# Second product of batch 2 as seven products of halves, and the whole list of steps in a new order

## The chip, the cores and the metric

One core of one Trainium2 chip. The metric is the device time of one execution in microseconds (us), the median of several runs. The core has a matrix engine (PE, with its weight loads shown apart as PEld), VectorE (DVE), ScalarE (ACT), GpSimd (POOL) and SyncE (SP), which only issues DMAs here. Each engine works through its own instructions in order; between engines only semaphores set the order.

## The reference

There are B = 8 batches of H = 8 heads, S = 512 tokens, 32 states, D = 64. Tokens read the states and states read the tokens, and the rows of both go through a two-layer network with a PReLU between.

```python
scores = scale * x @ state.T ; a = softmax(scores)  ; xread = a @ state
scores2 = scale * state @ x.T; a2 = softmax(scores2); sread = a2 @ x
rows = concat([xread, sread], axis=2)      # per batch 512 + 32 rows of d_model = 512
h = rows @ w_in                            # d_ff = 2048
g = maximum(h, 0) + alpha * minimum(h, 0)
out = g @ w_out                            # float32, 4352 x 512
```

## The kernel before

The kernel is a list of some 1,100 steps, the string `ORDER`. A step is a name with numbers, `F.5.12.2` for instance, and a small function is called for each. Every function puts instructions on one engine, so the list fixes the order on each of the five engines; there is no scheduler. A step waits for the data that it reads, and for the tile or PSUM bank that it writes to become free. PSUM banks are chosen in the list too: the last number of a PE step is one of six single banks, and a pair of banks named `two` holds the scores (`sc`) and some of the `m` products.

The token side needs no `xread`: since a @ state @ w_in = a @ (state @ w_in), the kernel forms m = state @ w_in once for each batch and then h = a @ m. Batch number 8 in the list is no batch of tokens: it holds the 32 state rows of all eight batches.

The steps, with b the batch:

- `lx`, `wi`, `wo`, `lst`: loads of x, w_in, w_out and the states, issued by POOL. `xd` (transposed x) and `tt` (transposed weights of a2) are DMA transposes, issued by SP. Batches 0 and 1 transpose x on PE (`xt`) and copy it out (`xo`); batch 0 takes its token weights through PE too (`tsc`, `at`, `ao`).
- `sc` (PE): scores into `two`. For the tokens: `sb` (DVE, transpose in blocks), `smax` (DVE), `ssh` (POOL or DVE, subtract), `sexp` (ACT), `ssum` (DVE), `snorm` (POOL), `wb` (DVE, back). After `wb` of its batch the first `F` can run. For the states: `tm` (DVE), `nb`, `te` (ACT), `tsum` (DVE), `tn` (POOL, two to a batch), `tt` (SP), `rd` (PE), `rdo` (copy). `te` is the last reader of the scores, and the next user of `two` waits for it.
- `m.b.f`: m for a quarter f of d_ff, `mo`: its copy to SBUF by ACT (`a`) or DVE (`v`).
- `F.b.j.k` (PE): a 128-wide chunk j of h, 16 to a batch, in bank k, two matmuls of 512 columns (four of 256 for batch 8). `N.b.j` (ACT): max(-h, 0). `G.b.j` (DVE): g = (1 - alpha) * N + h, which frees the bank. `f`, `n`, `g` are the same by half tokens, for the first four chunks of batch 0. `oma` is 1 - alpha.
- The second product in the plain form, for batches 0, 1 and 2: `S.b.q.i`, two of the sixteen matmuls of 512 columns that make one 128-row tile q of the output; `O.b.q`: its copy by ACT or DVE, and the DMA out from SP.
- The second product as seven products of halves (Strassen), for batches 3 to 8. g is cut in token halves and d_ff halves, w_out in d_ff halves and column halves. `W.i.c` (POOL, eight steps in all) forms the four sums of halves of w_out once. `U.b.i.c` (POOL) forms four sums of quarters of g, each in two parts c, eight steps to a batch; its tile has one buffer, so the sum of the next batch waits for the product that reads it. `P.b.p.i.c` (PE) are four matmuls of 256 columns, 28 such steps to a batch of tokens, in three banks px, py and pv. Products accumulate in px and intermediate states of it are kept: `K` (copy of px by ACT or DVE). `Q` (DVE, or a copy on ACT) adds a kept part to py or pv, and sends a quarter of the output.

```python
W_SUMS = {1: ((0, 1), (0, 0)), 3: ((1, 1), (0, 1)), 2: ((1, 1), 1), 4: ((1, 0), 2)}
# U: 1: g(1,c)+g(1,2+c)   2: U1-g(0,c)   3: g(0,c)-g(1,c)   4: g(0,2+c)-U2
```

In the trace the lines are: `F` L532 and L541 (batch 8), `S` L602, `P` L690, `m` L483, `sc` L298, `rd` L456, `N` L585, `G` L588, `U` L669, `W` L645, `K` L706, `Q` L721 and L723, `O` L619, `mo` L507 and L509, `te` L421, `tn` L435, `ssh` L367, `snorm` L384, `ssum` L380 and L381, `wb` L392, `sb` L329, `tm` L404.

Of the kernel before, what the change touches and what calls it, by code (L numbers as in the profile page):

```python
# [17 lines left out]
stc Z.0.9 wi.0 cx.0.1.a stt.0 sto.v Z.1.5 xt.0.0.1.1 lst sbd.0.v cx.0.0.a xt.0.0.0.2 xo.0.0.0.a cx.1.0.v cx.1.1.v  # L18
Z.3.6 xt.0.1.0.3 sbd.1.a lx.1 tsc.0.0.4 xo.0.0.1.v tsc.0.1 xt.0.1.1.5 sc.0.0 xo.0.1.1.a xo.0.1.0.v tsc.1.0.2 Z.0.2
tsc.1.1 smax.0.0 ssh.v.0.0 sexp.0.0 smax.0.1 ssh.v.0.1 sexp.0.1 sc.0.1 tm.0 Z.0.5 m.0.0.0.1 Z.3.11 oma mo.0.0.a.0  # L20
ssum.0.1 nb.0.a te.0.0 te.0.1 str.1.3 sro.1.a str.0.5 Z.4.13 wi.1 wo.0 snorm.p.0.1 at.1.4 ao.1.a ssum.0.0 snorm.p.0.0
sro.0.v wi.2 mo.0.0.v.1 m.2.0.2.0 mo.2.0.v.1 wo.1 m.1.0 mo.1.0.a at.0.3 ao.0.v xt.1.1.0.5 mo.2.0.v.0 wi.3 xo.1.1.0.a
xt.1.1.1.1 xo.1.1.1.v xt.1.0.1.4 xo.1.0.1.v f.0.1.1.0 n.0.1.1 g.0.1.1.1 xt.1.0.0.3 xo.1.0.0.v wo.2 f.0.0.0.2 n.0.0.0
g.0.0.0.0 m.1.1 mo.1.1.a m.0.1.5.1 mo.0.1.a.0 f.0.0.1.4 mo.0.1.a.1 g.0.1.1.0 f.0.1.0.3 W.1.0.p sc.1 n.0.0.1 n.0.1.0
g.0.0.0.1 tm.1 g.0.0.1.0 nb.1.a F.0.6.0 g.0.0.1.1 sb.1 g.0.1.0.1 N.0.6 G.0.6 g.0.1.0.0 F.0.5.2 te.1.0 lx.2 te.1.1
S.0.1.1.5 F.0.4.1 S.0.3.1.4 wo.3 S.0.3.0 S.0.1.0 m.0.2 F.0.7.0 N.0.4 G.0.4 N.0.5 G.0.5 mo.0.2.a N.0.7 S.0.2.1.3
S.0.2.0 G.0.7 F.0.9.1 tsum.1 tn.1.0 N.0.9 G.0.9 smax.1 ssh.p.1 xd.2 tsum.0 tn.0.1 F.0.10.2 S.0.3.3 N.0.10 G.0.10
S.0.1.3 tn.1.1 tt.1 S.0.1.2 F.0.8.0 F.0.11.1 N.0.11 N.0.8 S.0.3.2 G.0.8 m.0.3 S.0.0.0.2 G.0.11 S.0.2.3 S.0.0.3 S.0.0.2
mo.0.3.a tn.0.0 S.0.0.1 sexp.1 ssum.1 snorm.p.1 F.0.12.0 F.0.15.1 N.0.15 N.0.12 G.0.12 S.0.0.5 G.0.15 tt.0 S.0.0.4
S.0.1.4 m.1.2 S.0.1.5 wb.1 mo.1.2.a S.0.2.4 F.0.14.0 N.0.14 G.0.14 S.0.3.5 F.0.13.1 m.1.3 N.0.13 S.0.3.4 mo.1.3.a  # L30
F.1.3.0 N.1.3 S.0.0.7 G.0.13 S.0.0.6 O.0.0.a G.1.3 W.1.1.p F.1.4.1 N.1.4 G.1.4 S.0.2.6 F.1.2.2 N.1.2 F.1.0.0 N.1.0
G.1.2 S.0.1.6 S.0.1.7 O.0.1.a sc.2 G.1.0 tm.2 rd.0.1 m.2.2.2.5 rd.1.0 mo.2.2.a.0 W.2.0.p mo.2.2.a.1 S.0.2.2 F.1.1.2
F.1.8.5 rdo.0.v rdo.1.v nb.2.a te.2.1 N.1.8 sb.2 G.1.8 S.0.2.7 S.0.2.5 N.1.1 S.0.3.6 G.1.1 te.2.0 F.1.13.1 N.1.13 lx.3
tsum.2 S.0.3.7 O.0.3.a F.1.12.0 smax.2 F.1.6.5 G.1.13 O.0.2.a S.1.1.1.2 F.1.9.4 N.1.12 G.1.12 N.1.6 G.1.6 N.1.9
F.1.5.3 G.1.9 N.1.5 S.1.1.0 F.1.15.1 N.1.15 F.1.14.0 N.1.14 S.1.0.1.5 S.1.0.0 tn.2.0 ssh.p.2 tn.2.1 sexp.2 m.3.2
mo.3.2.a G.1.5 G.1.14 W.2.1.p m.3.0.4.3 mo.3.0.a.0 S.1.0.4 F.1.11.0 S.1.1.6 N.1.11 G.1.15 S.1.0.7 tt.2 mo.3.0.a.1
# [2 lines left out]
S.1.2.3.1 sb.3 smax.3 ssh.p.3 S.1.0.3 nb.3.a te.3.0 S.1.1.5 W.3.0.p F.2.0.0 N.2.2 te.3.1 rdo.2.v N.2.0 S.1.1.4 S.1.2.5
S.1.1.7 S.1.2.1 G.2.2 G.2.0 O.1.0.a O.1.1.a m.3.1 m.4.0.4.5 mo.4.0.a.1 m.4.1.3.2 tsum.3 mo.4.1.v.0 F.2.14.0 S.1.2.7  # L40
N.2.14 G.2.14 F.2.11.5 N.2.11 G.2.11 S.1.3.0.3 mo.4.1.a.1 S.1.3.7 F.2.9.0 S.1.3.3 mo.4.0.v.0 F.2.5.2 sexp.3 ssum.3
N.2.9 G.2.9 S.1.2.6 F.2.3.5 F.2.1.4 N.2.3 G.2.3 S.1.3.5 S.1.2.2 xd.4 mo.3.1.a S.1.3.4 N.2.1 G.2.1 N.2.5 G.2.5 F.2.8.0
lx.5 S.1.2.4 snorm.p.3 S.1.2.0 O.1.2.a wb.3 F.2.7.5 N.2.7 G.2.7 S.1.3.2 F.2.6.4 N.2.6 G.2.6 F.2.4.2 N.2.4 N.2.8
S.1.3.1 S.1.3.6 O.1.3.a F.2.10.1 sc.4 m.5.0.5.4 mo.5.0.a.1 mo.5.0.a.0 G.2.4 S.2.0.0.3 N.2.10 G.2.8 F.2.15.2 N.2.15
F.2.12.4 N.2.12 F.2.13.0 N.2.13 tm.4 F.3.9.5 G.2.10 G.2.15 S.2.0.1 G.2.13 nb.4.a S.2.2.0.1 W.3.1.p te.4.1 sb.4 W.4.1.p
te.4.0 S.2.0.4 S.2.2.5 N.3.9 G.2.12 xd.5 S.2.0.5 S.2.2.4 tn.3.0 tn.3.1 tt.3 tsum.4 m.4.2.2.0 mo.4.2.a.0 smax.4 ssh.p.4
# [1 line left out]
tn.4.1 F.3.10.5 N.3.10 G.3.10 m.5.2 mo.5.2.a rd.3.4 S.2.0.3 sexp.4 S.2.2.6 m.6.0 m.7.0.2.0 ssum.4 mo.7.0.a.1 S.2.0.6
O.2.0.a S.2.1.5.5 S.2.2.2 mo.7.0.a.0 F.3.2.0 N.3.2 G.3.2 F.3.6.3 rdo.3.a F.3.3.2 tn.4.0 tt.4 snorm.p.4 S.2.2.1 N.3.3
G.3.3 lx.6 N.3.6 F.3.8.4 F.3.0.0 S.2.2.7 F.3.11.2 G.3.6 S.2.1.4 S.2.1.2 N.3.8 G.3.8 N.3.0 G.3.0 mo.6.0.a m.5.3.3.4  # L50
N.3.11 sc.5 F.3.14.0 N.3.14 S.2.1.1 xd.6 O.2.2.v G.3.11 tm.5 F.3.4.1 mo.5.3.a.1 nb.5.a wb.4 te.5.1 mo.5.3.a.0 te.5.0
sb.5 N.3.4 G.3.14 S.2.1.3 F.3.5.2 S.2.3.2.4 W.4.0.p S.2.3.4 U.3.1.0.p G.3.4 N.3.5 G.3.5 smax.5 U.3.2.0.p U.3.4.0.p
S.2.3.3 S.2.3.6 S.2.3.7 S.2.1.0 rd.4.3 m.5.1 mo.5.1.a S.2.3.1 F.3.13.0 F.4.6.1 rdo.4.a N.3.13 G.3.13 N.4.6 F.4.1.2
F.3.12.3 S.2.3.0 G.4.6 N.3.12 N.4.1 G.4.1 G.3.12 lx.7 S.2.1.7 F.4.10.0 N.4.10 S.2.1.6 O.2.1.v F.4.4.1 N.4.4
P.3.1.1.0.2 ssh.p.5 sexp.5 P.3.1.0.1 U.3.1.1.p S.2.3.5 O.2.3.a U.3.2.1.p F.4.13.3 G.4.4 F.4.0.5 G.4.10 P.3.2.1.1.1
ssum.5 N.4.13 N.4.0 G.4.0 F.4.3.4 P.3.1.0.0 P.3.1.1.1 K.3.1.a P.3.2.0.1 P.3.2.0.0 G.4.13 N.4.3 U.3.4.1.p F.4.8.0 N.4.8
F.4.7.5 N.4.7 G.4.3 F.4.9.3 snorm.p.5 N.4.9 P.3.6.0.0 F.4.11.4 N.4.11 G.4.7 P.3.6.1.0 G.4.11 P.3.6.0.1 P.3.2.1.0
U.3.3.1.p G.4.8 P.3.6.1.1 K.3.2.a F.4.15.5 N.4.15 F.4.2.4 P.3.5.0.0 P.3.5.1.1 P.3.5.1.0 F.4.5.0 wb.5 G.4.15 P.3.5.0.1
G.4.9 Q.3.0.0 N.4.2 F.4.12.5 m.6.3.3.1 K.3.4.a P.3.3.1.0 G.4.2 U.3.3.0.p P.3.3.0.0 F.4.14.4 mo.6.3.v.1 N.4.12 G.4.12
P.3.3.1.1 N.4.5 G.4.5 N.4.14 G.4.14 mo.6.3.a.0 P.3.3.0.1 Q.3.0.1.a P.3.7.1.1.1 U.4.1.0.p U.4.2.0.p U.4.4.0.p U.4.1.1.p  # L60
m.6.2.5.0 mo.6.2.a.0 sc.6 sb.6 m.7.3.3.4 mo.7.3.a.0 m.6.1.2.5 mo.6.1.a.0 tm.6 mo.6.2.a.1 mo.6.1.a.1 P.3.7.0.0
P.3.7.1.0 P.3.7.0.1 Q.3.1.1 F.5.3.3 N.5.3 F.5.4.2 F.5.2.0 F.5.7.5 N.5.7 G.5.3 G.5.7 N.5.2 G.5.2 nb.6.a te.6.1 N.5.4
tsum.5 smax.6 G.5.4 P.3.4.1.1 P.3.4.0.0 P.4.1.1.1.3 P.4.1.1.0 F.5.14.5 N.5.14 P.4.1.0.0 P.4.1.0.1 K.4.1.a U.4.2.1.p
P.3.4.1.0 mo.7.3.a.1 P.3.4.0.1 F.5.10.0 N.5.10 F.5.13.2 N.5.13 G.5.14 F.5.1.4 G.5.10 G.5.13 tn.5.1 P.4.6.1.1 F.5.9.5
Q.3.1.0 N.5.9 tn.5.0 N.5.1 G.5.1 P.4.6.0.0 P.4.6.1.0 P.4.6.0.1 K.4.2.a P.4.2.0.0.0 te.6.0 F.5.11.2 G.5.9 tt.5 xd.7
ssh.v.6 N.5.11 G.5.11 F.5.0.1 N.5.0 F.5.15.4 P.4.5.1.0 P.4.5.0.1 N.5.15 G.5.15 F.5.8.5 U.4.3.1.p P.4.5.1.1 F.5.12.2
tsum.6 N.5.8 G.5.8 P.4.2.1.0 sexp.6 ssum.6 P.4.5.0.0 U.4.4.1.p F.5.6.4 G.5.0 P.4.2.0.1 P.4.2.1.1 K.4.4.a P.4.3.0.1
P.4.3.1.1 N.5.12 G.5.12 U.4.3.0.p P.4.7.0.0.5 N.5.6 F.5.5.1 P.4.3.1.0 P.4.3.0.0 Q.4.0.1.a snorm.p.6 U.5.1.0.p G.5.6
P.4.7.1.0 P.4.7.1.1 P.4.7.0.1 m.7.1.2.4 Q.4.0.0 wb.6 rd.5.0 sc.7 N.5.5 mo.7.1.a.0 rdo.5.a mo.7.1.a.1 G.5.5 m.7.2.3.1
mo.7.2.a.1 mo.7.2.a.0 F.6.8.2 Q.4.1.1 P.4.4.1.0 F.6.1.0 P.4.4.1.1 sb.7 N.6.1 G.6.1 F.6.12.4 F.6.3.1 N.6.3 F.6.6.3 tm.7  # L70
P.4.4.0.1 P.4.4.0.0 N.6.6 G.6.6 N.6.8 N.6.12 Q.4.1.0 P.5.1.0.1.0 nb.7.a te.7.1 tn.6.0 tn.6.1 tt.6 te.7.0 P.5.1.1.0
U.5.2.0.p G.6.3 G.6.8 U.5.1.1.p U.5.2.1.p P.5.1.0.0 tsum.7 P.5.1.1.1 K.5.1.a F.6.2.3 smax.7 tn.7.0 tn.7.1 P.5.2.1.0.5
# [702 lines left out]
```

## Time and profile before

| | us |
|---|---|
| median of 3 runs (lowest, highest) | 219.38 (219.21, 219.97) |
| the profiled execution | 219.88 |
| its span, first to last instruction | 218.1 |
| first matmul starts, last matmul ends | 1.33, 214.29 |
| busy: PE, DVE, POOL, ACT | 207.0, 171.5, 164.3, 144.4 |
| granted TensorE clock, mean | 0.998 |

"Busy" of PE counts each matmul to its modelled end, and neighbours overlap; so where the prediction speaks of PE's work it uses the distance from one matmul's start to the next one's when PE waits for nothing. An idle engine costs time only where another waits for what it does next.

### The profile page before, as it was taken

To read this page: it belongs to the slowest core of one execution; us is meant where nothing else is said; L and a number is where in the kernel's file an instruction comes from. 1 tells how busy PE (TensorE), PEld (TensorE's weight loads), DVE (VectorE), ACT (ScalarE), POOL (GpSimd) and SP (SyncE) were. 2 spreads that over 40 slices of the span, in tenths; PEclk is the share of its full clock that TensorE was granted. 3 is DMA by queue.
4 is the path that set the end of the run, shared out by engine and by line. 5 is a ranking of instruction groups with operands and counts; after the bars stand their busy time and mean duration, and the time that the engine had idled before them with its cause. 6 is when DMAs were issued, how large, how long until landed. Compare 5 with 4: busy or idle time off the path is not lost.

```text
span 218.1 us, 4862 instructions
## 1 busy us (share of the span) xinstructions
PE 207.0 (95%) x1931; PEld 128.3 (59%) x1931; DVE 171.5 (79%) x258; ACT 144.4 (66%) x279; POOL 164.3 (75%) x110
## 2 busy tenths in 40 slices
...
PEclk9999999999999999999999999999999999999999
...
GB/s 166 164 193 203 187 194 208 124 104 163 144 99 184 105 174 70 0 125 110 171 132 0 96 51 30 164 66 84 146 23 48 28 101 0 0 51 72 96 117 150
DMA packets 51927, 23.68 MB, mean 109 GB/s; under 512 B 38465, under 2 KB 50369, under 8 KB 51905
## 3 DMA queue, kind: packets, MB, share of 16 engines
...
q8 instruction: 15, 0.25, 0.4%
...
HBM read 17.31 MB, written 8.91 MB: 120 GB/s over the span
## 4 chain that ended last, share of the span: by engine, by line
PE 60%; DVE 10%; ACT 6%; issue 1%; ACTq 0%
PE px L690 17%; PE h L532 16%; PE pv L690 9%; PE o L602 7%; DVE g L588 5%; PE py L690 4%; PE h L541 3%; PE m_ps L483 3%; ACT e L421 2%; DVE ts L329 2%; ACT neg L585 2%; PE sr_ps L456 1%; DVE nb L404 1%; DVE ts L367 1%; PE sc L298 1%
## 5 line engine op out<-in xcount | busy, mean ns | idle before, releaser
L588 DVE SCALAR_TENSOR_TENSOR g<-neg,oma_sb,h 128x512 f16<-128x512 f32 (+1 forms) x140 | 93.5, 708 | 17.0 <-ACT neg L585 16.3
L585 ACT ACTIVATE neg<-h 128x512 f32<-128x512 f32 (+1 forms) x140 | 74.3, 581 | 28.0 <-PE h L532 18.2
L532 PE MATMUL h<-aT,m 128*128 128x512 f16 x248 | 67.5, 379 | 0.8 <-DVE g L588 0.5
L602 PE MATMUL o<-w_out_sb,g 128*128 128x512 f16 x192 | 49.9, 380 | 0.1
L690 PEld LDWEIGHTS <-gsum 128*128 128x128 f16 x352 | 34.2, 98 | 9.0 <-issue 0.5
L532 PEld LDWEIGHTS <-m 128*128 128x128 f16 x248 | 23.8, 98 | 23.3 <-issue 2.9
L602 PEld LDWEIGHTS <-g 128*128 128x128 f16 x192 | 17.6, 98 | 23.0 <-issue 3.1
L690 PEld LDWEIGHTS <-g 128*128 128x128 f16 x264 | 25.7, 98 | 6.5 <-DVE oq L723 0.3
L384 POOL TENSOR_TENSOR an<-ts,r 128x1024 f16<-128x1024 f32 (+1 forms) x9 | 15.4, 1720 | 16.3 <-DVE r L381 16.3
L669 POOL TENSOR_TENSOR gsum<-g 128x1024 f16<-128x1024 f16 (+1 forms) x12 | 24.4, 2047 | 0.8 <-PE pv L690 0.8
L669 POOL TENSOR_TENSOR gsum<-g,g 128x1024 f16<-128x1024 f16 (+1 forms) x12 | 23.5, 1962 | 1.5 <-DVE g L588 1.3
L669 POOL TENSOR_TENSOR gsum<-gsum,g 128x1024 f16<-128x1024 f16 (+1 forms) x12 | 23.6, 1965 | 0.9
L669 POOL TENSOR_TENSOR gsum<-g,gsum 128x1024 f16<-128x1024 f16 (+1 forms) x12 | 23.5, 1961 | 0.3
L690 PE MATMUL px<-ws,gsum 128*128 128x256 f16 x176 | 23.6, 273 | 0.0
L367 POOL TENSOR_TENSOR ts<-ts,mx 128x1024 f32<-128x1024 f32 x6 | 11.5, 1914 | 11.4 <-DVE mx L362 10.3
L706 ACT COPY kept<-px 128x512 f32<-128x512 f32 (+1 forms) x13 | 7.4, 569 | 18.1 <-PE px L690 13.6
L509 ACT CAST m<-m_ps 128x512 f16<-128x512 f32 x32 | 18.0, 602 | 1.6 <-PE m_ps L483 1.5
L435 POOL TENSOR_SCALAR e<-e,r 128x512 f16<-128x512 f16 x16 | 10.9, 688 | 8.9 <-DVE r L431 5.2
L483 PE MATMUL m_ps<-w_in_sb,stT 64*32 64x512 f16 x256 | 12.7, 383 | 2.9 <-ACT e L421 2.2
L723 DVE TENSOR_TENSOR oq<-pv,kept 128x512 f32<-128x512 f32 (+1 forms) x12 | 7.7, 643 | 8.7 <-ACT kept L706 4.4
L507 ACT CAST m<-m_ps 128x1024 f16<-128x1024 f32 x13 | 13.3, 1025 | 1.6 <-PE m_ps L483 1.6
L421 ACT ACTIVATE e<-sc,nb 128x512 f16<-128x512 f32 x16 | 11.0, 687 | 4.2 <-DVE ts L329 3.9
...
## 6 DMA issues: line engine op xcount, KB each, us to landing
...
w_out_sb<-in_moe_w_out_dram POOLq DMA_DIRECT2D x4, 512.0 KB, 12.0
...
```

Of the source, the lines that this page charges most:

```text
L367: engine(e).tensor_tensor(blocks(cols(live["ts", b], j, S)), blocks(scored(b, j)), over_blocks(cols(live["mx", b], j, S // N)), ALU.subtract,)
L384: engine(e).tensor_tensor(blocks(cols(live["an", b], j, S)), blocks(cols(live["ts", b], j, S)), over_blocks(cols(live["r1", b], j, S // N) ...
L421: nc.scalar.activation(live["e2", b][:, g, :, :], live["sc", b][:, :, :, g, :].rearrange("p r j s -> p (r j) s"), EXP, bias=live["nb", b][ ...
L483: nc.tensor.matmul(t[N * k : N * (k + 1), :], st_head(b, h)[64 * r : 64 * r + 64, :], w_in_sb[64 * r : 64 * r + 64, c, 512 * f : 512 * (f ...
L507: copier(e)(m_tile(b, f), t)
L509: copier(e)(m_tile(b, f)[:, g, :], t[g])
L532: nc.tensor.matmul(h.rearrange("p (r j s) -> p r j s", r=2, j=2), ms[b, f][:, g, 128 * j : 128 * (j + 1)], weights(b, g), start=(g == 0), ...
L585: nc.scalar.activation(neg, h, RELU, bias=0.0, scale=-1.0)
L588: nc.vector.scalar_tensor_tensor(g_tile(b, jc), negs.pop((b, jc)), oma_sb[:, jc : jc + 1], hs.pop((b, jc)), ALU.mult, ALU.add,)
L602: nc.tensor.matmul(outs[b, q], g_tile(b, jc)[:, 128 * q : 128 * (q + 1)], w_out_sb[:, jc, :], start=not begun and jc == 2 * jc2, stop=left ...
L669: engine(e).tensor_tensor(t, x(), y(), op)
L690: nc.tensor.matmul(pbanks[b, name][:, i, :], of(b, c)[:, j, 128 * i : 128 * (i + 1)], moving[:, 4 * c + j, :], start=not begun and j == 0, ...
```

## The change

`ORDER` alone is changed; all functions are as before. In batch 2 the 32 steps `S` and 4 steps `O` are left out, and 28 `P`, 8 `U`, 3 `K` and 4 `Q` put in their place. So 64 matmuls of 512 columns become 112 of 256, and POOL has eight sums more. `ssh.v.6` becomes `ssh.p.6`, that is, from DVE to POOL. Some copies go from ACT to DVE or back. All other steps are the same ones, but at other places in the list, some in other banks.

As an excerpt, the stretch in which batch 2's first product stands, before and after:

```diff
 ORDER = """
...
-F.1.7.1 N.1.7 S.1.0.2 ssum.2 G.1.11 F.1.10.4 N.1.10 snorm.p.2 m.2.1 G.1.7 xd.3 m.2.3.3.0 mo.2.3.a.1 mo.2.1.a
-mo.2.3.a.0 S.1.1.2 G.1.10 S.1.1.3 lx.4 m.3.3.1.0 rd.2.4 mo.3.3.a.0 sc.3 S.1.0.6 S.1.0.5 mo.3.3.a.1 wb.2 F.2.2.3 tm.3
...
-G.3.9 m.4.3 mo.4.3.a mo.4.2.a.1 S.2.0.7 S.2.2.3 F.3.1.4 N.3.1 F.3.15.2 G.3.1 N.3.15 G.3.15 S.2.0.2 F.3.7.0 N.3.7 G.3.7
...
+S.1.0.5 sc.3 m.4.0.1.5 mo.4.0.a.0 G.1.3 mo.4.0.a.1 W.3.1.p snorm.p.2 wb.2 lx.4 S.1.3.6.3 F.2.3.4 F.2.2.1 F.2.0.5
...
+F.2.5.5 mo.3.1.a F.2.11.2 S.1.3.4 S.1.3.3 S.1.2.1.0 S.1.1.3 N.2.11 G.2.11 rdo.2.a U.2.3.0.p N.2.5 xd.4 G.2.5 S.1.2.5
...
+mo.5.0.v.1 xd.5 m.4.2.1.0 mo.4.2.a.0 snorm.p.3 U.2.1.0.p U.2.2.0.p U.2.4.0.p wb.3 S.1.1.1 S.1.1.7 tsum.4 ssh.p.4
+S.1.1.4 F.3.9.2 F.3.7.3 mo.5.0.v.0 sexp.4 lx.6 P.2.1.1.1.1 mo.4.2.v.1 N.3.7 O.1.1.a ssum.4 P.2.1.0.0 N.3.9 G.3.7
...
+P.3.2.1.0 Q.3.0.0 P.4.2.0.0.2 P.4.1.0.0 K.4.1.a P.3.4.0.0 P.4.7.0.1.1 P.4.6.0.0 P.4.6.1.0 P.3.3.0.1 P.3.4.1.1
+P.4.6.1.1 P.4.6.0.1 ssum.6 P.4.2.1.0 snorm.p.6 P.4.2.0.1 P.3.3.1.1 ssum.5 snorm.p.5 Q.3.1.0 K.4.2.a P.4.5.1.1
+P.4.5.0.0 nb.6.a P.3.3.0.0 te.6.1 te.6.0 wb.6 F.6.3.0 wb.5 mo.6.1.a.1 Q.3.0.1.a P.4.2.1.1 P.4.5.0.1 Q.4.0.0 N.6.3
+G.6.3 U.4.3.0.p F.5.8.5 N.5.8 G.5.8 tsum.6 F.5.3.3 N.5.3 F.5.2.2 N.5.2 G.5.3 lx.7 F.5.7.0 N.5.7 G.5.2 G.5.7 P.4.5.1.0
...
+P.5.6.1.0 F.6.4.4 F.6.9.0 P.5.7.0.0 tn.7.1 K.5.2.v P.5.5.1.0 ssum.7 P.5.5.0.0 N.6.0 U.5.4.0.p N.6.9 G.6.9 P.5.5.1.1
+P.5.5.0.1 G.6.0 F.6.14.5 N.6.14 F.6.6.0 tt.7 rd.7.3 N.6.4 K.5.4.v Q.5.1.1 U.5.4.1.p P.5.3.0.1 G.6.4 P.5.3.1.1 G.6.14
...
 """
```

More of the change, by code (lines that the diff above doesn't have):

```diff
@@ L17 @@
 ORDER = """
[L18 to L36, printed above, removed]
-F.1.7.1 N.1.7 S.1.0.2 ssum.2 G.1.11 F.1.10.4 N.1.10 snorm.p.2 m.2.1 G.1.7 xd.3 m.2.3.3.0 mo.2.3.a.1 mo.2.1.a
@@ L38 @@
-mo.2.3.a.0 S.1.1.2 G.1.10 S.1.1.3 lx.4 m.3.3.1.0 rd.2.4 mo.3.3.a.0 sc.3 S.1.0.6 S.1.0.5 mo.3.3.a.1 wb.2 F.2.2.3 tm.3
[L39 to L46, printed above, removed]
-G.3.9 m.4.3 mo.4.3.a mo.4.2.a.1 S.2.0.7 S.2.2.3 F.3.1.4 N.3.1 F.3.15.2 G.3.1 N.3.15 G.3.15 S.2.0.2 F.3.7.0 N.3.7 G.3.7
@@ L48 @@
[L48 to L72, printed above, removed]
@@ L73 @@
-tt.7 F.6.11.1 N.6.11 G.6.11 P.5.2.1.1 P.5.6.0.1 P.5.6.1.1 G.6.12 F.6.14.2 N.6.14 G.6.14 F.6.9.1 N.6.9 G.6.9 ssh.p.7
-P.5.6.0.0 P.5.2.0.1 U.5.3.0.p N.6.2 G.6.2 F.6.7.4 N.6.7 P.5.6.1.0 G.6.7 sexp.7 P.5.2.0.0 F.6.15.2 rd.7.1 rdo.7.a
-rd.6.3 rdo.6.a K.5.2.v P.5.5.0.0 ssum.7 U.5.4.1.p F.6.4.4 F.6.5.1 F.6.10.3 P.5.5.1.1 Q.5.0.0 N.6.4 G.6.4 N.6.5 G.6.5
-U.5.3.1.p N.6.15 G.6.15 N.6.10 G.6.10 F.8.3.5 P.5.5.1.0 F.6.0.4 N.6.0 U.5.4.0.p P.5.5.0.1 K.5.4.a P.5.7.1.0.1 F.8.8.2
-N.8.8 G.8.8 P.5.7.0.1 F.6.13.3 G.6.0 N.6.13 P.5.7.1.1 P.5.7.0.0 P.5.3.1.0 P.5.3.1.1 snorm.p.7 P.5.3.0.1 U.6.1.0.p
@@ L93 @@
-U.8.3.1.p P.8.7.0.1 P.7.2.1.0 Q.7.0.1.a K.8.4.v Q.8.1.1 U.8.4.1.p P.8.3.0.1 P.8.4.0.0 Q.7.0.0 P.8.4.0.1 Q.8.1.0
-U.8.4.0.p P.8.3.0.0 Q.8.0.1.a
+Z.0.9 cx.0.1.a stc stt.0 sbd.0.v Z.1.5 xt.0.0.1.1 cx.0.0.a xt.0.0.0.2 Z.3.6 sto.v cx.1.0.v sbd.1.a xt.0.1.0.3
+xo.0.0.0.v tsc.0.0.4 xo.0.0.1.a cx.1.1.a tsc.0.1 xt.0.1.1.5 smax.0.0 wi.0 xo.0.1.0.a lst ssh.v.0.0 sc.0.0 xo.0.1.1.a
+tsc.1.0.0 Z.1.2 tsc.1.1 sc.0.1 smax.0.1 ssh.v.0.1 lx.1 wi.1 sexp.0.0 wo.0 wi.2 Z.1.5 m.0.0.1.2 tm.0 wi.3 Z.3.11
+mo.0.0.a.1 ssum.0.0 str.1.3 str.0.5 mo.0.0.a.0 Z.4.13 sexp.0.1 ssum.0.1 snorm.p.0.0 at.0.4 sro.1.v xt.1.1.1.0
```

79 lines of the change are left out of this document (64 added, 15 removed).

## The prediction

> **What bounds the kernel now.** First the page, for the shares:
>
> ```profile
> PE 207.0 (95%) x1931; PEld 128.3 (59%) x1931; DVE 171.5 (79%) x258; ACT 144.4 (66%) x279; POOL 164.3 (75%) x110
> PEclk9999999999999999999999999999999999999999
> ```
>
> PE is nearly always busy, at full clock. A share of 79% or 75% elsewhere may hide full stretches, so next the windows: us from the start; busy us (and instructions) of PE, PEld, DVE, ACT, POOL.
>
> ```profile
> 0.00:25.00 25.00, 21.24 (x257) 13.43 (x257) 17.72 (x35) 15.13 (x28) 14.31 (x21) 1.00 1.13 180
> 25.00:50.00 25.00, 23.67 (x211) 10.28 (x211) 19.83 (x30) 19.20 (x36) 11.91 (x9) 1.00 1.11 163
> 50.00:75.00 25.00, 24.67 (x207) 10.30 (x205) 22.65 (x33) 21.46 (x40) 15.66 (x11) 1.00 0.87 145
> 150.00:175.00 25.00, 25.00 (x249) 18.91 (x247) 22.90 (x36) 17.20 (x37) 24.54 (x14) 1.00 0.21 54
> 98.30:212.40 114.10, 113.21 (x1040) 83.31 (x1039) 89.54 (x133) 67.77 (x137) 108.73 (x61) 1.00 0.31 75
> ```
>
> From the first `U` (98.30) to the last (212.39) POOL is idle for only 114.1 - 108.7 = 5.4 us. DVE is about 90% busy from 50 on. ACT and POOL have room early only. Then the chain, for what a matmul step takes when PE waits for nothing (start us, us):
>
> ```profile
> 69.03 0.86 PE o L602 x4
> 200.32 1.75 PE px L690 x16
> 212.98 0.87 PE pv L690 x8
> 213.85 0.45 PE px L690 x4
> ```
>
> 0.86 / 4 = 0.216 us for 512 columns, 1.75 / 16 = 0.109 for 256. Last the groups by form, for the steps that change in number (busy us, mean ns):
>
> ```profile
> L690 PEld LDWEIGHTS <-gsum 128*128 128x128 f16 x352 | 34.2, 98 | 9.0 <-issue 0.5
> L588 DVE SCALAR_TENSOR_TENSOR g<-neg,oma_sb,h 128x512 f16<-128x512 f32 x124 | 86.9, 738 | 13.3 <-ACT neg L585 12.7
> L669 POOL TENSOR_TENSOR gsum<-g,g 128x1024 f16<-128x1024 f16 x10 | 21.2, 2124 | 1.3 <-DVE g L588 1.3
> L723 DVE TENSOR_TENSOR oq<-pv,kept 128x512 f32<-128x512 f32 x10 | 6.9, 687 | 8.1 <-ACT kept L706 4.4 <-PE pv L690 3.6
> ```
>
> Adding all PE steps of the list at such distances (`F` and `S` 0.432, `P` 0.436, `m` 0.35, `Z` 0.109 each, the rest likewise) gives 199.8 us of work. The last matmul ends at 214.29, so PE has waited 14.5 us (1.33 of it before its first matmul); the tail to the span's end is 3.8 (last copy, output DMA). 199.8 + 14.5 + 3.8 = 218.1. The profiled execution took 219.88, 1.78 more than its span; the median of the runs, 219.38, is 1.28 above the span, and that is what I add at the end. A change is measurable here from about 0.3%, 0.66 us.
>
> **The change, engine by engine.** PE loses 64 x 0.216 = 13.8 and gains 112 x 0.109 = 12.2: its work is 198.2, less by 1.6, the most that the change itself can bring while PE stays the bound. The distance of 0.109 bears the weight loads, 98 ns each, because they run under the matmul before. The Trainium skill ("TensorE: Matmul & The Clock Gate", Part 3) says that a weight load overlaps running matmuls only where the row group differs; all row groups are used here. By that rule the 112 would take 112 x (0.098 + 0.109) = 23.2 us and batch 2 would lose 9.4; this trace runs 616 such matmuls at 0.109, against it.
>
> POOL gains 8 x 2.12 = 17.0 and `ssh.p.6` 1.9: busy 164.3 to 183. All `W` must now be done before batch 2; POOL was idle 13.1 and 9.3 us between 25 and 75, so these cost nothing. DVE trades copies with ACT; counted through, with one `ssh` of 2.1 less and three `Q` sums of 0.69 more, it gains 0.7, and ACT loses 0.6. Of the DMAs on POOL's queue `lx.7` moves latest, to 121.7 us of PE's work: load (6.6) and transpose (3.9, on SP) take 10.5, and `sc.7` comes 14.3 later, so 3.8 to spare. On SP's queue the transposes `tt` stand behind output DMAs as before; all are over 4 us ahead of their `rd` but two: `tt.2`, which its `tn` releases early, and `tt.7` (rival D).
>
> The rest is order. I added up, for each engine, the work that stands in the list ahead of a place, DVE and ACT at the distances of busy neighbours (`G` 0.67, `N` 0.51):
>
> - ahead of the first 20.3 us of PE's work: old DVE 23.2, ACT 18.7; new 22.6 and 22.5
> - ahead of 40.4: old 37.9, 34.3; new 40.7, 38.4
> - ahead of 60.3: old 58.7, 53.3; new 60.0, 58.1
> - ahead of 100: old 94.6, 89.0; new 98.5, 91.0
>
> So the new list wants `F` steps earlier, to feed POOL, and its front asks more of DVE and ACT.
>
> *Front.* I followed the new order by hand with the rows' durations. It is as before up to the first `F`. Then `te.1`, `N.0.6`, `mo.0.2.a`, three `N`, `sexp.1` and `mo.0.3.a` stand in one row on ACT, and `m.1.2` waits for the last of them: it comes at about 31.8 us with 21.2 of PE's work done, 10.6 waited. At `F.1.0.0` it is 43.0 us and 10.7; the old order has waited 9.9 there. Half of the gain is gone at 43 us.
>
> *Middle.* A PE step that reuses a bank waits for the `G` or copy that frees it. What PE has waited there is DVE's idle time so far, plus DVE's work ahead less PE's work ahead. Check on the old list: `F.2.14` waits for `G.2.0`, work difference -2.7, DVE idle until 67.6 us by windows 14.3: 11.6, and PE had waited 11.1. At `m.6.3` on `Q.3.0.0` (120 us): -6.5 + 19.9 = 13.4, actual 13.2. New list: DVE idle at 45 us 10.3 by hand (old 11.6), then as in the old, 10.6 us in the 100 from 50 to 150. The tightest places are `m.4.1` on `G.2.11` (-0.6, 69 us): 12.2 waited; `F.3.15` on `G.3.13` (-1.1, 90 us): 14.0; `m.6.1` on `mo.7.3` (-3.6, 122 us): 14.9; `F.6.8` on `G.6.11` (-7.1, 158 us): 15.2. From there the old list loses nothing more to speak of. If DVE, asked sooner, idles at four fifths of that rate, it is 13.2 (at `m.6.1`); if ACT starves it up to 69 us as it was between 25 and 50 (5.2 us idle in 25), 2.4 more, 17.6. I take 15.2, the old rate, since it held for 100 us.
>
> *Sum.* 198.2 + 15.2 + 3.8 = 217.2 against 218.1; 219.38 - 0.9 = 218.5.
>
> **The rivals.**
>
> A, the forecast: 218.5. For it: PE's work follows from counts alone (48 matmuls more, in the halved form), so that the change does what it says is no question here; and the sum over DVE fits the old run at both places.
>
> B, no change: the front and middle cost all of the 1.6, PE waits 15.5 to 16.7; 219.4. For it: 0.8 is gone by 43 us already.
>
> C, slower: POOL takes over as the bound. From `U.2.1.0` on, free at about 71.5 us (its last `F` ends at 57.8 of PE's work, + 11.8 waited + 1.9 for `N` and `G`), POOL has 132.2 us of work. In the old run the last matmul ended 1.9 after the last `U`; for A, POOL must end at 211.5. That leaves 211.5 - 71.5 - 132.2 = 7.8 us of idle time; the old rate (5.4 in 114.1) gives 6.6. The rival decides from 7.8 on. Every `U` here waits for a `G` or a product that comes just in time, and the `snorm`, `tn` and `ssh` of four batches stand in the same queue; before 98 us the old POOL waited for DVE over 30 us in all:
>
> ```profile
> POOL an L384 <- DVE r L381: 16.3, 6, 5.6
> POOL ts L367 <- DVE mx L362: 10.3, 3, 5.8
> ```
>
> With 10.5 us idle, POOL ends at 214.2, the span at 219.9, and the time is 221.2. Against it: in the old run `U` steps themselves waited for `G` only 1.3 us.
>
> D, slower too: a transposed weight comes late. `rd.7.3` stands in the list right behind `tt.7`; in the old list 5.2 us of PE's work lie between. `tn.7.1` ends about 12.0 us of POOL work after `U.5.1.1` starts (four sums, two `tn`, `ssh`); that starts at the earliest at 148.0, and the transpose lands 3.4 us after its issue: 163.4, where PE arrives at 149.7 + 14.8 = 164.5. It costs from a delay of 1.1 us on; on PE `F.8.13` and the products of batch 5 are queued behind it, and for those `N`, `G` and POOL's next sums. A delay of 4 us gives 217.2 + 2.9 + 1.28, or 221.4.
>
> E, each weight load of batch 2 adds its 98 ns in the open: 112 x 0.207 - 13.8 = 9.4 more, 228.8. This is the rule of the Trainium skill named above; batches 3 to 7 speak against it.
>
> **The numbers.** A 0.44; B 0.17; C 0.25; D 0.13; E 0.01. Faster by over 0.3% is A, 0.44; within 0.3% B, 0.17; slower C, D and E, 0.39. The time is A's. The range: below, A with 13.2 waited, 198.2 + 13.2 + 3.8 + 1.28 = 216.5; above, C and D with their prices, 221.4, which takes in 17.6 waited (220.9). A's own range is 216.5 to 218.7.
>
> **What would show it.** In the changed profile: the last matmul near 213.4; `m.1.2` near 32 us; the first `U` near 66 us and POOL idle under 7.8 us from 71.5 to the last `U`, which ends 1.9 before the last matmul; few waits of PE or PEld on POOL. Wrong would be: gaps before `P` steps that end with a gsum, or PE idle before the last `rd` (C, D); a longer idle time of DVE between 45 and 90 us with the first `U` after 70 (B); a distance of 0.2 us in batch 2's products (E).

## The result and the profile after

The changed kernel takes 213.47 us (median of 4 runs, 213.35 to 213.94), the kernel before 219.68 beside it: ratio 0.972, 95% interval 0.970 to 0.975. It is 6.2 us faster. The prediction had the direction, but 218.5 us and a range down to 216.5: the gain is far larger than the forecast.

The profiled execution took 213.49 us, its span is 211.7. The page, for the shares:

```profile
PE 202.8 (96%) x1979; PEld 133.1 (63%) x1979; DVE 173.0 (82%) x259; ACT 144.0 (68%) x280; POOL 182.0 (86%) x119
...
PEclk9999999999999999999999999999999999999998
...
PE 90%; DVE 5%; DMA 2%; issue 0%; ACT 0%; POOL 0%; DVEq 0%
```

The third line is the chain that ended last, by engine, in shares of the span: for 90% of the span it runs over PE's own work. The windows (busy us and instructions of PE, PEld, DVE, ACT, POOL):

```profile
0.00:25.00 25.00, 20.18 (x254) 13.07 (x255) 16.78 (x33) 17.48 (x34) 13.46 (x22) 1.00 1.14 185
25.00:50.00 25.00, 24.72 (x188) 10.50 (x187) 23.95 (x34) 21.42 (x41) 18.93 (x12) 1.00 1.06 162
50.00:75.00 25.00, 25.00 (x256) 10.99 (x255) 24.40 (x33) 23.04 (x46) 23.06 (x15) 1.00 1.04 151
150.00:175.00 25.00, 25.00 (x212) 18.02 (x211) 22.97 (x37) 16.91 (x34) 24.03 (x14) 1.00 0.22 65
63.78:205.68 141.90, 141.90 (x1376) 101.89 (x1375) 117.39 (x172) 91.52 (x181) 137.11 (x78) 1.00 0.40 86
```

From the first `U` (63.78) to the end of the last (205.68) PE has no idle time at all. DVE rose from 19.83 to 23.95 us between 25 and 50, and from 22.65 to 24.40 between 50 and 75. POOL is idle 4.8 us between first and last `U`. The chain, for the distances (start us, us):

```profile
67.36 2.16 PE o L603 x10
...
196.55 1.75 PE px L691 x16
...
206.60 0.89 PE pv L691 x8
```

They are the old ones, 0.216 and 0.109 us, so PE's work is 198.2 as worked out. The last matmul ends at 207.91: PE has waited 9.7 us, not 14.5 as before. Of the 6.4 us by which the span is shorter, 1.6 are PE's work and 4.8 PE's waits. 9.3 of the 9.7 lie ahead of `m.1.2` at 30.47 us; behind it PE waits for almost nothing. The groups by form:

```profile
L691 PEld LDWEIGHTS <-gsum 128*128 128x128 f16 x416 | 40.4, 98 | 9.8 <-issue 0.7
...
L589 DVE SCALAR_TENSOR_TENSOR g<-neg,oma_sb,h 128x512 f16<-128x512 f32 x124 | 85.8, 738 | 4.6 <-ACT neg L586 2.9 <-PE pv L691 0.6
...
L670 POOL TENSOR_TENSOR gsum<-g,g 128x1024 f16<-128x1024 f16 x12 | 25.5, 2127 | 1.2 <-DVE g L589 0.8 <-PE px L691 0.4
...
L724 DVE TENSOR_TENSOR oq<-pv,kept 128x512 f32<-128x512 f32 x12 | 8.2, 682 | 9.0 <-PE pv L691 5.1 <-ACT kept L707 3.9
```

No operation became cheaper. What changed is idle time: ahead of the 124 `G` it was 13.3 us and is 4.6. DVE's waits on ACT ahead of all 140 `G`, those of batch 8 among them, before and after (us in total, times, longest):

```profile
DVE g L588 <- ACT neg L585: 16.3, 26, 2.2
```

```profile
DVE g L589 <- ACT neg L586: 6.1, 15, 0.8
```

Where do the `G` come from earlier? From PE: its matmuls of the first product `F` alone, in 30 to 45 us, before and after:

```profile
30.00:45.00 15.00, 5.46 (x20) 1.00 1.15 162
```

```profile
30.00:45.00 15.00, 8.01 (x30) 1.00 0.92 149
```

In the traces 16 `F` steps have started by 45 us before, 22 after; by 105 us 61 and 69. (Some of the expectations below say 18 and 24: they count two more for the four half-token steps `f`.) Both PEs are fully busy in this stretch; the old one runs second products instead. Output tiles (from their first matmul to the end of their copy) hold 3.67 of the six single banks on average from 30 to 45 us before, 2.83 after; `F` tiles hold 1.81 and 2.49. The two go together; that the banks are the reason for the earlier `F` was not tested.

### The profile page after: what moved, and what is told of

Its sections match the earlier page's. It is cut to its first block, busy times and chain, and to the rows that moved or that the text cites. A ratio compares the mean times of both kernels' runs of the same rounds, so it can differ in the third digit from the quotient of the medians.

```text
span 211.7 us, 4977 instructions
## 1 busy us (share of the span) xinstructions
PE 202.8 (96%) x1979; PEld 133.1 (63%) x1979; DVE 173.0 (82%) x259; ACT 144.0 (68%) x280; POOL 182.0 (86%) x119
## 4 chain that ended last, share of the span: by engine, by line
PE 90%; DVE 5%; DMA 2%; issue 0%; ACT 0%; POOL 0%; DVEq 0%
PE h L533 25%; PE px L691 21%; PE o L603 13%; PE pv L691 11%; PE py L691 5%; PE m_ps L484 4%; PE h L542 3%; PE z L220 3%; PE sr_ps L457 2%; DMA st<-in_state_dram 2%; DVE g L574 2%; PE sc L299 1%; PE xT_ps L284 1%; PE st_ps L231 1%; DVE g L589 1%; DVE m L508 1%
## 5 line engine op out<-in xcount | busy, mean ns | idle before, releaser
L691 PEld LDWEIGHTS <-gsum 128*128 128x128 f16 x416 | 40.4, 98 | 9.8 <-issue 0.7
L603 PE MATMUL o<-w_out_sb,g 128*128 128x512 f16 x128 | 33.2, 379 | 1.1 <-DVE g L574 1.1
L670 POOL TENSOR_TENSOR gsum<-g,g 128x1024 f16<-128x1024 f16 (+1 forms) x14 | 27.8, 1988 | 1.6 <-DVE g L589 0.8
L670 POOL TENSOR_TENSOR gsum<-gsum,g 128x1024 f16<-128x1024 f16 (+1 forms) x14 | 27.8, 1988 | 0.9
L670 POOL TENSOR_TENSOR gsum<-g,gsum 128x1024 f16<-128x1024 f16 (+1 forms) x14 | 27.7, 1990 | 0.3
L691 PE MATMUL px<-ws,gsum 128*128 128x256 f16 x208 | 27.1, 273 | 0.0
L368 POOL TENSOR_TENSOR ts<-ts,mx 128x1024 f32<-128x1024 f32 x7 | 13.4, 1911 | 6.9 <-DVE mx L363 6.9
L691 PE MATMUL pv<-ws,gsum 128*128 128x256 f16 x104 | 15.0, 273 | 0.0
L691 PE MATMUL px<-w_out_sb,g 128*128 128x256 f16 x104 | 14.8, 273 | 0.0
L691 PE MATMUL px<-w_out_sb,gsum 128*128 128x256 f16 x104 | 14.5, 273 | 0.0
L691 PE MATMUL py<-w_out_sb,g 128*128 128x256 f16 x104 | 14.5, 273 | 0.0
```

What stands on the lines that cost most here:

```text
L368: engine(e).tensor_tensor(blocks(cols(live["ts", b], j, S)), blocks(scored(b, j)), over_blocks(cols(live["mx", b], j, S // N)), ALU.subtract,)
L603: nc.tensor.matmul(outs[b, q], g_tile(b, jc)[:, 128 * q : 128 * (q + 1)], w_out_sb[:, jc, :], start=not begun and jc == 2 * jc2, stop=left ...
L670: engine(e).tensor_tensor(t, x(), y(), op)
L691: nc.tensor.matmul(pbanks[b, name][:, i, :], of(b, c)[:, j, 128 * i : 128 * (i + 1)], moving[:, 4 * c + j, :], start=not begun and j == 0, ...
```

## The experiments

All times are medians. "Before" ran beside every kernel, at 219.8 to 220.0 us; the new list is the changed kernel, 213.5. Line numbers differ by a few from kernel to kernel.

### The two parts of the change

**The new list, batch 2 plain.**

```diff
-P.2.1.1.1.1 ... U.2.* K.2.* Q.2.*
+S.2.0.4.1 ... (32 S on the 28 places and four behind) O.2.0.a O.2.1.a O.2.2.v O.2.3.v
```

> The new list with the second product of batch 2 plain again: its 28 product steps become 32 steps of whole rows at the same places (four more behind the last), the eight half sums, the three kept copies and the four quarter outputs of batch 2 go, four row copies come in; the first eight groups of g of batch 2 lie in the space of the half sums, which are free until then. Theory (the gain is 1.6 us of TensorE work plus some 4.6 us of single TensorE waits that the new list no longer has): only the 1.6 us come back, 213.5 + 1.6 = 215.1 us, at most 215.8; TensorE's waits stay near 9.7 us. Rival (the seven products themselves took the waits away, the list is only their carrier): the waits come back too, 218 us or more.

219.23 us, a ratio of 0.998: nearly all of the gain seems gone, as the rival has it. But the waits of PE are new ones:

```profile
PE px L697 <- POOL gsum L676: 1.8, 2, 1.0
...
PE px L697 <- ACT kept L713: 1.2, 1, 1.2
```

`U.3.1.0` waited for the last plain step, because the experiment had put batch 2's `g` into its space. So the run can't decide about the products. With the `g` in other space:

> As the first run with batch 2 plain, but its first eight groups of g lie in two half sums of later use and in two of the kept copies, so that no half sum of batch 3 has to wait for the last plain step (there U.3.1.0 began at 107.5 us instead of 100.6, and TensorE lost 3.05 us behind it). Theory (VectorE's line is the second bound, and the new list has it busy from 17 us on: idle 1.2 us from 17 to 45 us instead of 4.5; plain steps need less of VectorE than the products): only TensorE's work of 1.6 us comes back, 214.8 to 215.6 us. Rival (without the products the list's waits come back): 217 us or more.

215.61 us (ratio 0.982, 0.980 to 0.984), at the upper edge of the theory: PE waits 10.0, against 9.7 with the products. So the order alone brings 4.2 us and the products 2.1 on top of it: 1.6 of PE's work, 0.3 of waits in the two traces, and 0.2 that is within the spread of the runs.

The DVE of this run, the third engine of the row, from 45 to 150 us:

```profile
45.00:150.00 105.00, 104.52 (x989) 58.19 (x988) 95.64 (x132) 81.45 (x158) 79.65 (x48) 1.00 0.63 109
```

It is idle 9.4 us, and yet PE has only 0.5 us of idle time in this stretch. The new list with the products has DVE idle 6.7 us there, the old list 11.4 (rows further down). So DVE's idle time by itself is not the price: the difference to the new list is work that the plain form doesn't ask for (95.6 us busy against 98.3).

**The old list with the products.**

```diff
-S.2.0.0.3 ... S.2.3.5 O.2.*  W.3.1.p W.4.1.p W.4.0.p (at 75 to 98 us)
+P.2.1.0.0.1 ... P.2.4.1.1 U.2.* K.2.* Q.2.*  W.3.1.p W.4.0.p W.4.1.p (by 65 us)
```

> The old list with the second product of batch 2 as seven products on 28 of its 32 old places; eight half sums on GpSimd as soon as their g halves are there, five weight sums moved ahead into GpSimd's old idle time before 75 us. Theory (products alone bring 1.6 us of TensorE work, and the old list has no room on GpSimd: its idle time from 80 to 96 us is 9.5 us, the sums need 17.1 less one weight sum of 2.1, so all later half sums come 5.4 us later): no gain, 220 to 223 us, with waits on GpSimd. Rival (the products themselves free the engines): 213.5 to 216 us.

The edit moves three weight sums (the expectation's text says five). 224.84 us (1.023), beyond the theory: PE has waited 21.1. Its waits and POOL's:

```profile
PE px L690 <- POOL gsum L669: 2.1, 2, 1.8
```

```profile
POOL gsum L669 <- DVE g L588: 5.6, 2, 5.0
```

POOL stands 5 us for the `G` that the sums need and is late from there. In an order that makes `G` late the products cost 5 us; in the new order they bring 2.

### Which piece of the order?

**PE's waiting steps moved, in the old list.**

```diff
-m.4.2.2.0 ... m.4.3 mo.4.3.a mo.4.2.a.1 S.2.0.7 S.2.2.3 F.3.1.4
+m.4.2.2.0 ... mo.4.2.a.1 S.2.0.7 S.2.2.3 F.3.1.4 m.4.3 mo.4.3.a
```

and six more of the kind. The quarter (1,1) of batch 3 then takes in `P.3.4.1.1`, which belongs behind it, so that its output is not the right one; only the time is read.

> The old list, batch 2 plain, with seven TensorE steps moved by a few places so that the steps that waited come later or others stand ahead of them (m.4.3 behind F.3.1, S.1.2.7 before m.4.1, S.1.2.6 before F.2.14, F.5.12 behind P.4.5.0.0, S.2.3.1 before m.5.1, S.2.3.0 before F.4.1, P.3.4.1.1 before P.3.7.0.0). These waits sum to 3.6 us in the profile of before. Theory (each wait is a step that stands too early for its bank or its copy; PE's waits are no debt to VectorE): 2.5 to 3.2 us faster than before, 216.5 to 217.2 us, and VectorE's idle time after 45 us falls. Rival (the prediction's premise: PE's wait follows VectorE's idle rate, so a wait removed comes back at the next step): less than 1 us, 218.7 us or more.

219.59 us (0.999, 0.998 to 1.000): nothing, and my theory of single waits fell. The waits that were removed are gone from the trace, and others stand a few steps on: PE has waited 11.1 at 70 us and 13.4 at 130 before, 11.0 and 13.6 here. DVE's idle time from 45 to 150 is 11.4 and 11.8.

**DVE's load, in both lists.** Three reductions of 1.2 us more:

```diff
+nc.vector.tensor_reduce(dummy, w_in_sb[:, 0, :1024], AX.X, ALU.max)   # at three places
```

> The new list with three more reductions on VectorE (a maximum over 1024 elements of the first weights into a scalar that nobody reads, about 1.2 us each) at about 50, 62 and 85 us. VectorE is idle 0.83 us from 45 to 85 us and 6.7 us from 45 to 150 us in the profile after. Theory (TensorE is the bound, VectorE's work lies ahead of its need by more than a step): under 0.8 us slower, under 214.3 us. Rival (VectorE's line is as full as TensorE's, its work lies just in time): each comes through, 2.5 to 3.6 us slower, 216 to 217.1 us.

> The old list with the same three reductions on VectorE as in the new list's run, at about 51, 65 and 85 us. VectorE is idle 11.4 us from 45 to 150 us in the profile of before. Theory (VectorE's idle time there is time in which nothing is ready for it; what it does, TensorE waits for): 2.5 to 3.6 us slower, 222.3 to 223.4 us. Rival (VectorE follows TensorE's and ScalarE's pace, the idle time takes the work in): under 1 us slower, under 220.8 us.

New list 215.95 us, 2.5 slower: the rival's lower edge. Old list 221.06, 1.3 slower (1.007, 1.005 to 1.008), between both theories: only the first of the three came through, 1.0 of 1.2 us. Three token maxima made short:

```diff
-nb, live["sc", b].rearrange(...), AX.XY, ALU.max
+nb, live["sc", b].rearrange(...)[:, :, :, : 32 if b in (2, 3, 4) else 128], AX.XY, ALU.max
```

> The old list with the token maxima of batches 2, 3 and 4 taken over a quarter of the scores each (the maximum only shifts the exponentials): some 0.9 us less for each on VectorE, 2.6 us in all, at about 45, 61 and 79 us. Theory (VectorE's line sets TensorE's waits): 1.6 to 2.6 us faster, 217.2 to 218.2 us. Rival (banks and the places of TensorE's steps set them): under 0.5 us, 219.3 us or more.

> The new list with the same three token maxima over a quarter of the scores. Theory (TensorE doesn't wait after 31 us, VectorE's line is just in time but not late): at most 0.3 us faster, 213.2 us or more. Rival (VectorE's line still sets the time somewhere): 1 us or more faster, under 212.5 us.

Old list 218.85 us, 0.9 faster (0.997) for 2.4 less (a shortened maximum took 0.42 us, a whole one 1.21), between theory and rival; new list 213.46, no change, as the theory had it. So the new list has DVE's work just on time: more costs, less gives nothing. In the old list DVE is one of several limits.

**The readers of the scores.** One view of the old list, the timeline around the scores of batch 4 (start us, us; in brackets the idle time before):

```profile
81.89 0.69 ACT L421 ACTIVATE e<-sc,nb 128x512 f16<-128x512 f32 x1
...
82.70 1.25 DVE L329 STREAM_TRANSPOSE ts<-sc 128x1024 f32<-128x1024 f32 x1
...
83.98 0.69 ACT L421 ACTIVATE e<-sc,nb 128x512 f16<-128x512 f32 x1 [1.32 <-DVE ts L329]
...
84.81 0.41 PE L483 MATMUL m_ps<-w_in_sb,stT 64*32 64x512 f16 x8 [0.97 <-ACT e L421]
```

`te`, `sb`, `te` read the same bank pair in turn, ACT waits 1.32 us for DVE, and `m.4.3` on PE for the last of them. The new list has `sb` next to `tm`, ahead of both `te`. The Trainium skill ("PSUM — Partial Sum Buffer", PSUM bank collisions raise a hardware error) says that two engines must not use one bank in the same partitions at once, two reads included, and that software has to keep them apart. The trace agrees: here they follow each other to within 0.04 us. That order moved into the old list, and the old order into the new:

```diff
-tm.4 ... nb.4.a ... te.4.1 sb.4 ... te.4.0       (old list; 1, 2, 3 and 5 likewise)
+sb.4 tm.4 ... nb.4.a ... te.4.1 ... te.4.0
```

> The old list with one kind of step moved: VectorE's block transpose of the scores (sb) of batches 1 to 5 stands next to the token maximum (tm), ahead of ScalarE's two exponentials (te) of the same scores, as it does in the new list. In the profile of before the three readers of one score tile never overlap: te.4.1, sb.4 and te.4.0 follow each other to within 0.04 us, ScalarE idle 1.32 us ahead of te.4.0, 1.24 ahead of te.1.0 and 1.09 ahead of te.3.0, VectorE idle 0.85 us ahead of sb.2 and 1.09 ahead of sb.5; the profile after has no such idle time. Theory (these turns put ScalarE and VectorE behind, and TensorE waits for both later): 1.5 to 3.5 us faster, 216.3 to 218.3 us. Rival (as with the moved TensorE steps, what is won here is lost at the next hand-over): under 0.5 us, 219.3 us or more.

> The old list with sb first as in the run beside it and with the TensorE steps of the mended list moved too (without P.3.4.1.1). Theory: with the readers' turns gone the moved steps pay as well, 0.5 to 1.5 us below the run with sb first alone, 215.5 to 217.5 us. Rival: no more than that run, within 0.4 us of it.

> The new list with the old order of the readers for batches 2, 4 and 5: sb behind the first exponential (2 and 4) or behind both (5), and the maximum over blocks (smax) behind it. Theory (the readers' turns are a main part of what the old list lost): 1.5 to 3.5 us slower, 215.0 to 217.0 us. Rival (the new list has the room to take them in): under 0.5 us, 214 us or less.

Old list with `sb` first: 219.16 us, 0.7 faster (0.998, 0.996 to 0.999), between rival and theory; with six of the PE steps moved as well 220.05, no gain (1.001) and 0.9 slower than `sb` first alone, which neither text expected. At 80 us the wait only changes its name: `S.2.2.0` now waits 1.08 us for the `G` that stands behind `sb` and `tm`, where `m.4.3` waited 1.16. New list with `sb` late: 217.08, 3.6 slower, just beyond the theory and far from the rival. But this edit moves more than the readers. `smax` reads what `sb` wrote, so it moves too, and the weights of the batch hang on it. The waits of this run that name the turns at the score tile are small (us in total, times, longest):

```profile
ACT e L421 <- DVE ts L329: 1.3, 1, 1.3
...
DVE ts L329 <- ACT e L421: 0.6, 2, 0.5
```

Meanwhile `sexp.2`, the exponentials that lead to batch 2's weights, starts at 52.64 us instead of 49.84, 2.8 later. So 3.6 us is the price of late readers and of the late token softmax behind them; the run does not part the two. What the new list can't do without hardly helps the old one.

**Joined lists.** If the lead at 45 us (22 `F` steps against 16) were the thing, it could be handed to the old order. The banks behind the joint were given out anew, so a control goes with them.

```diff
+ORDER = new list up to 45 us + the old list's order for all other steps   (and old + new; new up to 64 us + old)
```

> The new list up to 45 us (its first 24 first products of batches 0 and 1), then the old list's order for all that is left, batch 2 plain; behind 45 us each tile takes the bank that was released longest ago. Theory (the gain is the lead that VectorE gets by 45 us): 3 to 4 us faster than before, 215.8 to 217.0 us. Rival (the order behind 45 us decides): 218.8 us or more.

> The old list up to 45 us (18 first products), then the new list's order for all that is left, batch 2 as seven products; banks behind 45 us as in the run beside it. Theory (the lead by 45 us is missing, VectorE's line is full from there on): 3 to 4 us slower than the new list, 216.5 to 217.8 us. Rival (the order behind 45 us decides): under 214.5 us.

> The new list up to 64 us (its first half sum), then the old list's order, batch 2 plain. Theory: no worse than the join at 45 us, 215.4 to 217.0 us. Rival: 218.5 us or more, if the old order behind 64 us brings its own waits back.

> Control: the old list, same order of all steps, with the banks behind 45 us assigned by the same rule as in the joined lists (145 steps get another bank). Theory (the order and not the choice of banks sets the time): within 0.7 us of before, 219.1 to 220.5 us. Rival (the old list's banks are what held it up): 1 us or more faster.

New then old at 45 us: 219.31 us, 0.7 faster (0.997); at 64 us: 219.04, 1.0 faster (0.995). Old then new: 220.09, no gain at all, slower than both texts had it. Control: 221.03, 1.0 slower (1.004), 0.5 past the theory's edge; some of the gain of the two joins may be hidden by that. The lead theory fell too: with these banks the old order does not keep the lead. PE's `F` matmuls in the first of these:

```profile
30.00:45.00 15.00, 8.01 (x30) 1.00 0.92 151
45.00:65.00 20.00, 4.46 (x17) 1.00 0.85 135
```

By 65 us it has started 30 `F` steps, as many as the old list, and DVE has sat idle 4.1 us from 45 to 65, where it was 1.3 before. What it had won it gave back as idle time. DVE from 45 to 150 us (third of the five), before, after and here:

```profile
45.00:150.00 105.00, 102.81 (x958) 55.63 (x953) 93.57 (x128) 83.72 (x162) 79.38 (x48) 1.00 0.56 106
```

```profile
45.00:150.00 105.00, 105.00 (x1057) 64.87 (x1055) 98.28 (x136) 84.13 (x165) 98.69 (x58) 1.00 0.62 110
```

```profile
45.00:150.00 105.00, 102.84 (x938) 55.62 (x936) 90.90 (x123) 81.84 (x159) 75.02 (x46) 1.00 0.57 107
```

In the other direction 2.5 of the 6.6 us lost against the new list are the joint's own: `sb.2` and `smax.2` came to stand ahead of `G.1.13`, and PE waited 2.48 us for it. But the new order also wants its DVE work sooner than the old front has delivered it: PE waits 2.7 us more between 45 and 70.

### The limits of the new list

**POOL.** One half sum twice:

```diff
-U.2.1.0.p U.2.2.0.p
+U.2.1.0.p U.2.1.0.p U.2.2.0.p
```

> The new list with one half sum (U.2.1.0) computed twice in a row on GpSimd, 2.1 us more at about 66 us; the next 85 us have 2.2 us of GpSimd's idle time. Theory (TensorE is the bound, GpSimd's sums lie ahead of their products by a microsecond or more): under 0.7 us slower, under 214.2 us. Rival (rival C of the prediction: GpSimd's line is full behind 70 us, what comes late stays late to the last sum): 1.5 to 2.1 us slower, 215.0 to 215.7 us.

215.45 us, 2.0 slower for 2.1 more: the rival. But not by the last sum. The timeline of this run:

```profile
79.61 1.92 POOL L368 TENSOR_TENSOR ts<-ts,mx 128x1024 f32<-128x1024 f32 x1
...
81.56 1.06 ACT L377 ACTIVATE ts<-ts 128x1024 f32<-128x1024 f32 x1 [2.46 <-POOL ts L368]
...
83.62 0.59 PE L533 MATMUL h<-aT,m 128*128 128x512 f16 x2 [1.34 <-ACT osb L620]
```

`ssh.4` comes late behind the sums, `sexp.4` on ACT waits 2.46 us for it, the copy `O.1.1` stands behind `sexp.4`, and PE waits for the bank that it frees. Behind 85 us PE waits for nothing more.

**The front.** Two tries for a faster kernel.

```diff
-m.2.0.5.0 ... mo.2.0.a.1 mo.2.0.a.0 ... sb.1 g.0.1.1.1 ... g.0.1.1.0 ... smax.1 G.0.6 G.0.5
+g.0.1.1.1 g.0.1.1.0 sb.1 ... G.0.6 G.0.5 smax.1 ... S.0.1.4 m.2.0 mo.2.0.a
```

> A try for a faster kernel. The new list with its front changed: m.2.0 and its copy go from 18 us to about 35 us (0.35 us of TensorE and 1.2 of ScalarE in the stretch where both copying engines are full), the two partial prelu steps that S.0.1.1 waits 1.23 us for stand ahead of sb.1, the exponentials te.1 ahead of N.0.5, smax.1 behind G.0.5, the one-less-alpha step at 9 us. Theory (from 17 to 30 us VectorE is idle 0.11 us, so only order and ScalarE can give): 0.3 to 1.0 us faster than the new list, 212.5 to 213.2 us. Rival (smax.1 and with it the weights of batch 1 come too late): 0.5 us slower or more, over 214 us.

216.63 us, 3.2 slower, in the rival's range, but mostly by another path than the one that it named. With `sb.1` behind the two `g`, `te.1` came late and `m.0.2` waited 1.7 us for it; `m.1.2` waited 1.2 us for a copy on ACT. The second try keeps the order and shortens the token maxima of batches 0 and 1, as for batches 2 to 4 above:

> The new list with the token maxima of batches 0 and 1 over a quarter of the scores (the maximum only shifts the exponentials): 0.9 us less for each on VectorE, at about 12.6 and 21.4 us. Theory (in the front VectorE is the bound: idle 0.11 us from 17 to 30 us): 0.6 to 1.2 us faster than the new list, 212.3 to 212.9 us. Rival (the front's waits are hand-overs, as most of the old list's): under 0.3 us, 213.2 us or more.

213.04 us (0.970, 0.968 to 0.972), the fastest of all and 0.4 below the new list, between theory and rival; but its interval overlaps the new list's. The wait at `S.0.1.1` went from 1.23 to 0.85 us, so DVE's load is a part of the front's waits and not all.

## Why the prediction was wrong

**PE's work, -1.6: right.** 0.216 and 0.109 hold, the 112 more weight loads of 98 ns stayed under the matmuls. Rival E did not occur.

**POOL gains 17.0 + 1.9: right.** 182.0 busy against the 183 worked out; the tail is 3.8 as said.

**Front, 10.6 waited at `m.1.2` (31.8 us): too much, and by a path that was not taken.** It was 9.3 at 30.47 us, `F.1.0` at 41.6 us with 9.4 instead of 43.0 with 10.7. `m.1.2` did not wait for ACT's row at all (start us, us; the last copy of the row, then the `F` step ahead of `m.1.2`, then `m.1.2`):

```profile
29.40 0.99 ACT L508 CAST m<-m_ps 128x1024 f16<-128x1024 f32 x1
...
29.95 0.59 PE L533 MATMUL h<-aT,m 128*128 128x512 f16 x2
...
30.47 0.41 PE L484 MATMUL m_ps<-w_in_sb,stT 64*32 64x512 f16 x8
```

The copy `mo.0.3` ended at 30.39, and `m.1.2` followed the `F` step ahead of it at the usual distance of 0.52 us. The waits of the front lie earlier: by 28.64 us nearly all of it had been waited. The longest near the end is the one ahead of `S.0.1.1`, which stood 1.23 us for a half-token `g` on DVE.

**Middle, the sentence "PE's wait is DVE's idle time so far, plus DVE's work ahead less PE's work ahead": it holds where PE is held by DVE. "As in the old, 10.6 us in the 100 from 50 to 150": the step that failed.** DVE's measured idle time put into the same sentence gives 9.74 - 0.6 = 9.1 at `m.4.1`, 10.1 - 1.1 = 9.0 at `F.3.15`, 12.7 - 3.6 = 9.1 at `m.6.1`, 16.5 - 7.1 = 9.4 at `F.6.8`; PE had waited 9.3 to 9.45 at all four. I had 12.2, 14.0, 14.9 and 15.2. The sentence is an account of time: it is exact where a PE step stands waiting for DVE, gives a lower bound elsewhere, as here, and says nothing of why DVE is idle. One of its two checks on the old list was misread: DVE was idle 13.5 us until 67.6, not 14.3, so the sentence gives 10.8 against the 11.1 waited; the other check comes out. DVE was idle 9.3 us by 45 us instead of 10.3, and from there to `F.6.8` 7.3 us in 107, 6.8 in 100. The old rate had "held for 100 us", and I took it for a property of DVE. It goes with the list: 11.4 us in 105 in the old one, 9.4 in the new order with batch 2 plain, 6.7 in the new one whole. The prediction's own table said that the new list asks 2.8 us more of DVE ahead of the first 40 us of PE's work and 3.9 ahead of the first 100, and that is a list that leaves it less time to be idle. Why this order lets DVE work so early is argued here (earlier `F`, more banks for them), not shown. The lower end of the range, "four fifths of that rate", did not reach it.

**The sum.** 218.5 - 213.5 = 5.0 too much: 5.5 of PE's waits (1.3 in the front, 4.2 in the middle), less 0.5 because the median stands 1.8 above the profiled span, not 1.28.

**The rivals.** B did not occur: DVE idle from 45 to 90 us was 1.5 us instead of 4.6, and the first `U` ran at 63.8. C did not occur: the last `U` ends 2.2 ahead of the last matmul. From 71.5 us to the last `U` POOL is idle 4.3 us; the 7.8 from which C decides belong to an end at 211.5, and the last `U` ended at 205.68, so the two can't be set side by side. Its worry was sound: POOL is nearly full in this stretch, and 2.1 us more on it cost 2.0. D did not occur: `rd.7.3` ran at 159.15 without a wait. Yet the rivals looked only for what could go wrong; none was "the waits go away".

**What stays open.** Shown are the split, 4.2 us order and 2.1 products; that in the new list the order of the scores' readers, with the token softmax that hangs on it, is worth 3.6 us; that no piece taken into the old list gave more than 1.0 us (the front up to 64 us), and less work on DVE 0.9; and that a lead is lost again under the old order. How the 4.2 us divide over the pieces was not found, and the control with other banks, 1.0 slower, limits what the joined lists say. How much of the 3.6 us is the readers' turns themselves, and how much the later weights, is open too. That they work only together is argued from these runs, not shown by one.
